# Attention into a feed-forward block on one core: the values product with its operands exchanged, a column of ones beside V, and the stages reordered

## The chip, the cores and the metric

The kernel runs on one core of one Trainium2 chip. The metric is the device time of one execution in microseconds (us), as a median of several runs. A profile of one execution tells what each engine did: TensorE (PE, with its weight loads as PEld), VectorE (DVE), ScalarE (ACT), GpSimd (POOL), and the queue of SyncE (SP), which issues transfers.

## What is computed

Eight batches, 12 heads, 448 positions, head size 64. Queries and keys are normalised, attended, the heads are joined to rows of 768, and each row goes through two products with a sine term between them.

```python
# q, k, v: (8, 12, 448, 64) f32; w_in (768, 2048), w_out (2048, 768), alpha (2048)
q_n = q / sqrt(mean(q*q, -1) + 1e-6) * g_q           # k_n likewise with g_k
scores = (q_n @ k_n^T) / 8
attn = exp(scores - max); attn /= sum(attn, -1) + 1e-9
x = (attn @ v) -> rows of 12 * 64 = 768               # 3584 rows
h = x @ w_in
out = (h + sin(alpha * h)**2 / alpha) @ w_out
```

The kernel leaves out the subtraction of the maximum before and after the change alike.

## The kernel before

**Tiling.** One batch is a stage (loop over `b`, L628). A batch's 12 heads are three groups `c` of four heads (two pairs of two). The 448 positions are cut as 64 rows x 7 (`j`), so that a tile always fills 128 partitions with two heads. A group of q and k is called `ci = 3 b + c`.

**The steps of a stage.** For each group: load q and k (`l`, L155), square them (`q`, L274, ACT for the first two groups, POOL later), sum the squares (`u`, L288, DVE), take the inverse root as Ln and Exp (`r`, L292, ACT), fold g in (`g`, L283, POOL), scale (`k`, L302, DVE for the first four groups, POOL later) and transpose to `qkT`: by PE and copies (`p`, L323) for the first groups, by DMA transposes on SP (`t`, L315) later. A token `S` is one tile of scores (L348): four 64x64 matmuls of 448 columns into a pair of PSUM banks, and one Exp on ACT into `expT`. There are 21 a stage. They hold keys on the partitions and queries along the columns.

**Values and sums.** `attend` (L385) multiplies with V (or a tile of ones, for the sums) as the weights and 448 columns of `expT` as the moving side. Its result is x already turned, head dimension on the partitions. Group 0 takes 64-column weights for the values (`v`), and for the sums (`o`) 32 columns of ones over half of the queries in batches 1 to 7 (L404). Groups 1 and 2 go together with 32-column weights: sums (`x`), even and odd columns of V (`y`, `z`; L416). The sums become reciprocals as Ln and Exp(-) on ACT (L423 to L432; group 0's halves are also moved across partitions by DVE, L429), and DVE multiplies them into `xT` (L440).

**The two products.** `first_product` (L460) multiplies the six 128-row blocks of `xT` (`kt`) by w_in, 16 blocks `m` of the 2048, 448 columns each. Its first four `m` are interleaved over the blocks in the order 0, 1, 2, 4, 3, 5. Each pair of `m` then passes `snake` (L443): Sin on ACT, square on POOL (even `m`) or ACT, and on DVE the sum into `g_sb` (L454). `second_product` (L498) of batch b - 1 runs inside stage b as fillers: it has 6 or 8 units, each of 8 fills, a fill being 8 matmuls of 64x64 weights and 384 columns in four quadrants (L548); at a unit's end DVE copies and adds (L554, L555) and SP stores. The last batch's second product runs alone at the end, on the whole array (L529).

**What sets the order.** The plans STAGE_0, STAGE_1 and STAGE_N (batches 2 to 7) are lists of tokens, written out by hand, and each engine works its instructions in that order. A number or `f` is that many fills, `f` from the second open unit. The dictionary of a plan holds tokens that are issued beside the first product, by its step (-1: within the interleaved part). A string of digits gives the pair of PSUM banks (of four) to each tile in turn. `W`, `O` and `V` are loads of w_in, w_out and V, all on POOL's queue, which casts them to bf16. An `S` with a number has that many warm-up matmuls on a blank tile before it (L352).

Of the kernel before, what the change touches and what calls it, by code (L numbers as in the profile page):

```python
# [17 lines left out]
try:  # L18
# [15 lines left out]
        "q000 u000 q010 G q011 q001 u010 g00 u011 r01 g01 D1 u001 k01 r00 k00 q11 u11 O00 q10 V00 p012 "  # L34
        "W01 q20 p00 g1 u10 r1 q21 u20 V01 g2 S4 V02 S k11 l3 k10 S1 S1 S4 W00 W02 S u21 r2 p1 L S2 S q31 "
        "S3 k21 q30 k20 D2 S S3 o3 l4 g3 S W10 W12 o1 o3 p2 u30 l5 S3 u31 S1 S W11 S4 v7 S S S q40 S S x5 "
        "y3 q41 u41 x1 g4 z4 u40 x1 r4 y4 O01 q50 z3 r3 O10 "
    ),
    "012311203203312021021302301231032103021321302",
    {-1: 'u50 O11 k30', 0: 'D4 k401', 1: 'k411', 2: 'q51', 3: 'k31 k400 u51', 5: 'k410', 7: 'g5 V12', 8: 't3 V10 V11 t4 l6 l7'},  # L40
# [3 lines left out]
        "4 r2 f f k20 1 f f 2 k21 S 1 q31 1 t2 S 1 S 2 S q30 2 S 2 S S 3 f S 3 S 1 f S 1 S 1 u31 2 l5 g3 "  # L44
        "S u30 o1 o6 1 r3 V10 2 S f q41 1 f 2 S 2 S 2 q40 S u41 1 v1 v1 S v3 V12 S k31 q50 v2 u40 S 2 S "
        "V11 g5 S z4 x7 y7 r4 z3 g4 k30 "
    ),
    "1320201203203013133213130101301231203123",
    {-1: 'u50 t3', 0: 'k41', 2: 'k40', 5: 'q51', 6: 'l6 t4', 8: 'u51 l7'},
# [3 lines left out]
        "f q40 f 1 f 2 q41 1 S 1 r2 5 f S f f S 2 S 1 u40 k20 1 k21 S 1 u41 1 S 2 S 1 q31 1 o7 1 f f 1 S "  # L53
        "t2 f 1 r4 S 2 f 1 l5 q30 S 3 S 1 u31 1 S 2 u30 g3 V10 S 2 S S k41 3 S v6 r3 k30 S k31 v1 S 2 V12 "
        "g4 2 S 2 S 2 q51 l6 S t3 z3 x7 y5 y2 z4 V11 "
    ),
    "01223131310312323203013012301021310231023",
    {-1: 'k40', 0: 't4', 2: 'q50', 3: 'u50', 4: 'u51 g5', 6: 'l7'},
)
LAST = "0123012"  # L60


def tokens_of(plan):

    return [t for word in plan.split() for t in ("F" * int(word) if word.isdigit() else [word])]
# [3 lines left out]
def kernel(  # L69
# [12 lines left out]

# [24 lines left out]
    vpool = ctx.enter_context(tc.tile_pool(name="vpool", bufs=2))  # L115
    npool = ctx.enter_context(tc.tile_pool(name="norm", bufs=2))
    tpool = ctx.enter_context(tc.tile_pool(name="qkT", bufs=8))
    epool = ctx.enter_context(tc.tile_pool(name="expT", bufs=17))
    hpool = ctx.enter_context(tc.tile_pool(name="parts", bufs=1))
    rpool = ctx.enter_context(tc.tile_pool(name="rec", bufs=2))  # L120
    xpool = ctx.enter_context(tc.tile_pool(name="xT", bufs=1))
# [6 lines left out]

# [3 lines left out]
    upcoming = deque()  # L132
# [11 lines left out]
    qk, vb, norm = {}, {}, {}  # L144

    def strip(pp, hi):

        s = 2 * hi + pp
        return slice(s * 32, s * 32 + 32)

    def half_of(c, pp, hi):

        return pp ^ (hi, 1, 0)[c]

    def load_qk(ci, k_queue=nc.sync):  # L155

# [17 lines left out]
    def load_v(b, c):  # L174


        if b not in vb:
            vb[b] = vpool.tile([P, NP, NJ, D], BF16, tag="vb", name="vb")
        heads = v[b].rearrange("(n pp) (p j) d -> n pp p (j d)", pp=2, j=NJ)
        rows = vb[b].rearrange("p n j d -> p n (j d)")  # L180
        if c == 1:
            for r in range(2):
                nc.gpsimd.dma_start(out=rows[r * 64:r * 64 + 64, 1:4], in_=heads[1:4, 1 - r].rearrange("n p x -> p n x"))
        else:
            n = slice(0, 1) if c == 0 else slice(4, NP)
            nc.gpsimd.dma_start(out=rows[:, n], in_=heads[n].rearrange("n pp p x -> (pp p) n x"))
# [15 lines left out]
    ones = const.tile([P, D], BF16)  # L202
    nc.vector.memset(ones, 1.0)
    ones_row = const.tile([1, P], F32)
    nc.vector.memset(ones_row, 1.0)
    eps = const.tile([P, 1], F32)
# [13 lines left out]
    def spread_g():  # L220

        nc.gpsimd.tensor_mul(g_rows[:, 2], g_rows[:, 0], g_rows[:, 1])
        ps = bank_pair("gps")
        nc.tensor.matmul(ps[:, 0, :D], ones_row, g_rows[:, 2], start=True, stop=True)
        nc.vector.tensor_copy(gg[:, 0], ps[:, 0, :D])
        give_back(ps)

    def spread_alpha():

        ps = bank_pair("aps")  # L230
        nc.tensor.matmul(ps[:, 0, :MT], small, ident_f32, start=True, stop=True)
        nc.vector.tensor_copy(alpha_sb[:, :, 0], ps[:, 0, :MT])
        give_back(ps)
        nc.vector.reciprocal(inv_alpha_sb, alpha_sb)

    def load_w_in(half, c):


        cols = slice(half * D_FF // 2, (half + 1) * D_FF // 2)
        rows = moe_w_in[c * 2 * P:(c + 1) * 2 * P, cols]  # L240
        nc.gpsimd.dma_start(out=w_in_sb[half][:, 2 * c:2 * c + 2],  # L241
                            in_=rows.rearrange("(p x) f -> p x f" if c else "(x p) f -> p x f", x=2))

    def load_w_out(hi, lo):
        src = moe_w_out.rearrange("(mt p) d -> p mt d", p=P)
        part = 2 * hi + lo
        mts = slice(part * MT // 4, (part + 1) * MT // 4)
        nc.gpsimd.dma_start(out=w_out_sb[:, mts], in_=src[:, mts])  # L248

    def keep_busy(n, rhs):  # L250


# [7 lines left out]
    def norm_tasks(ci):  # L260

        st = SimpleNamespace()
        early = ci <= NC
        st.ms = npool.tile([P, 2, 2 * NJ], F32, tag="ms", name="ms")
        st.inv, st.inv_ps, st.scaled = {}, [], 0
        st.sq, st.n = {}, None
# [5 lines left out]
        def square(w, heads=(0, 1)):  # L274
            if ci < 2:
                st.sq[w] = spare(2 * ci + w).rearrange("p (a d) -> p a d", d=D)
                rows = slice(heads[0] * NJ, (heads[-1] + 1) * NJ)
                nc.scalar.activation(st.sq[w][:, rows], qk[ci][:, w, rows], ACT.Square)  # L278
            else:
                st.sq[w] = npool.tile([P, 2 * NJ, D], F32, tag="sq", name="sq")  # L280
                nc.gpsimd.tensor_mul(st.sq[w], qk[ci][:, w], qk[ci][:, w])  # L281
# [10 lines left out]
        def rsqrt(ws=slice(0, 2)):  # L292
            ln = npool.tile([P, 2, 2 * NJ], F32, tag="inv", name="inv")
            inv = bank_pair("inv") if early else ln
            if early:
                st.inv_ps.append(inv)
            for w in range(2)[ws]:
                st.inv[w] = inv[:, w, :2 * NJ]
            nc.scalar.activation(ln[:, ws], st.ms[:, ws, :], ACT.Ln, scale=1.0 / D, bias=eps)
            nc.scalar.activation(inv[:, ws, :2 * NJ], ln[:, ws], ACT.Exp, scale=-0.5)  # L300

        def scale(w, heads=(0, 1)):  # L302
            eng = nc.vector if early else nc.gpsimd
# [20 lines left out]


# [22 lines left out]
    def scores(c, j, warm=0):  # L348

# [3 lines left out]
        for pp in range(2):  # L353
            for hi in range(2):
                qkt, r = qkT[2 * c + pp], slice(hi * 64, hi * 64 + 64)
                o = half_of(c % NC, pp, hi) * 64
# [6 lines left out]
    avs, recs = {}, {}  # L363
    presums = {}

    def add_tile(b):


        if b not in presums:
            presums[b] = SimpleNamespace(n=0, t=rpool.tile([P, 2, S], F32, tag="rec", name="rec"))  # L370
        s = presums[b]
        first = expT[b * NC, 0] if s.n == 0 else s.t
        s.n += 1
        nc.vector.tensor_add(s.t, first, expT[b * NC, s.n])

    def split_sum(b):

        s = presums[b]
        assert s.n == NJ - 1
        s.parts = [hpool.tile([P, 2, S], BF16, tag=f"part{i}", name="part") for i in range(2)]  # L380
        nc.vector.tensor_copy(s.parts[0], s.t)
        nc.vector.tensor_sub(s.parts[1], s.t, s.parts[0])
    STEPS = {"o": "ones 0", "v": "values 0", "x": "ones 1", "y": "low 1", "z": "high 1"}

    def attend(b, what, tiles=range(NJ)):  # L385

        kind, both = what.split()
        both = both == "1"  # L390
        if tiles[0] == 0:
            avs[what] = bank_pair("av")
        av = avs[what]
        pre = presums.get(b) if what == "ones 0" else None
        last = 1 if pre else NJ - 1
        halved = what == "ones 0" and b > 0
        for j in tiles:
            if halved:
                for hi in range(2):
                    for qh in range(2):  # L400
                        for pp in range(2):
                            r = half_of(0, pp, hi) * 64
                            r, o = slice(r, r + 64), slice((2 * pp + qh) * 32, (2 * pp + qh) * 32 + 32)
                            nc.tensor.matmul(av[o, hi, :S // 2], ones[r, :D // 2], expT[b * NC, j][r, hi, qh * S // 2:(qh + 1) * S // 2],  # L404
                                             start=(j == 0), stop=(j == NJ - 1))
                continue
            for hi in range(2):
                for c in ((1, 2) if both else (0,)):
                    for pp in range(2):
                        r = half_of(c, pp, hi) * 64  # L410
                        r = slice(r, r + 64)
                        o, k = (strip(pp, hi), c - 1) if both else (slice(pp * 64, pp * 64 + 64), hi)
                        d = slice(kind == "high", D, 2) if both and kind != "ones" else slice(D // 2 if both else D)
                        w = ones[r, d] if kind == "ones" else vb[b][r, 2 * c + hi, j, d]
                        x = pre.parts[j] if pre else expT[b * NC + c, j]
                        nc.tensor.matmul(av[o, k, :S], w, x[r, hi, :], start=(j == 0), stop=(j == last))  # L416
        if tiles[-1] < last:
            return
        if kind == "ones":
# [261 lines left out]
```

The softmax here doesn't subtract the row's maximum and nothing guards it: scores larger than these inputs give would overflow.

## Time and profile before

| | us |
|---|---|
| median of three runs | 407.25 (407.24 to 407.7) |
| span of the profiled execution, first to last instruction | 405.8 |
| PE busy in the span | 391.4 |
| ACT | 315.3 |
| POOL | 283.6 |
| DVE | 240.6 |

The profiled execution's span is counted from its first to its last instruction; the median of the runs is 1.45 us longer, and holds what lies around the span. Busy times are sums over the span. Matmuls are pipelined, so two that overlap are counted once; a start of a matmul and the start of the next tell more than its duration. The profile's page has the shares by slices of the span, groups of instructions by line, and a chain: the work that ended last, followed back from the end, each step to what released it. In the table of windows each row is a stretch of the span with the busy time of each engine. A weight load (PEld) and a matmul (PE) are separate instructions. The costliest groups are the two products (L548 148.0 us of PE, L468 147.0), the exps (L360, 143.7 us of ACT) and DVE's part of the sine term (L454, 81.1).

### The profile page before, as it was taken

What the parts mean: (1) busy time and instruction counts of PE and PEld (TensorE: products, weight loads), DVE (VectorE), ACT (ScalarE), POOL (GpSimd) and SP (SyncE); (2) the same over time, 40 slices, a digit from 0 to 9 for tenths busy, and PEclk for the clock granted to TensorE, in tenths of its full rate; (3) what the DMA queues carried; (4) which work ended last, traced back from release to release, by engine and by line L of the source; (5) the groups of instructions that cost most, each with busy time, mean ns of one, the idle gap of its engine ahead of it and who ended that gap; (6) DMA issues with size and microseconds to landing.
All of it is one profiled execution on the core that took longest, in us unless ns stands there. A gap on an engine that the chain in (4) does not pass through costs nothing.

```text
span 405.8 us, 15218 instructions
## 1 busy us (share of the span) xinstructions
PE 391.4 (96%) x6755; PEld 238.8 (59%) x6758; DVE 240.6 (59%) x364; ACT 315.3 (78%) x474; POOL 283.6 (70%) x268
## 2 busy tenths in 40 slices
PE   1999999999999999999999999999999999999996
PEld 1346467645675566755676556755667556765564
DVE  4956665756783576638584475836685485544512
ACT  5798889868896879958898678958898679877600
POOL 5998889987959789588877779597895784003300
PEclk9999999999999999999999999999999999999999
DMA  7999999855286925697076923879046901620022
GB/s 266 215 254 241 210 221 255 193 155 171 53 164 162 151 94 88 182 198 153 3 140 178 200 102 70 185 158 209 3 94 179 166 2 22 108 61 1 2 78 79
DMA packets 67846, 55.46 MB, mean 137 GB/s; under 512 B 41524, under 2 KB 63172, under 8 KB 67780
## 3 DMA queue, kind: packets, MB, share of 16 engines
q1 hardware_dynamic: 56578, 41.43, 42.2%
q0 software_dynamic: 10432, 11.81, 19.0%
q8 instruction: 53, 0.87, 0.9%
q10 hardware_dynamic: 770, 1.25, 0.9%
q14 instruction: 13, 0.11, 0.1%
HBM read 45.62 MB, written 11.01 MB: 140 GB/s over the span
## 4 chain that ended last, share of the span: by engine, by line
PE 88%; POOL 5%; DMA 3%; issue 1%; DVE 1%; ACT 1%; SPq 0%; POOLq 0%
PE hps L468 34%; PE ops L548 31%; PE av L416 9%; PE sc L357 7%; PE ops L529 5%; POOL sq L281 2%; DMA qk<-in_q_dram 2%; DMA qk<-in_k_dram 2%; PE av L404 1%; POOL qk L286 1%; POOL w_out_sb L248 1%; POOL w_in L241 1%; ACT expT L360 1%; DVE g_sb L454 0%; DVE xT L440 0%
## 5 line engine op out<-in xcount | busy, mean ns | idle before, releaser
L360 ACT ACTIVATE expT<-sc 128x896 bf16<-128x896 f32 x168 | 143.7, 917 | 7.4 <-PE sc L357 6.6
L548 PE MATMUL ops<-w_out_sb,g_sb 64*64 64x384 bf16 x3072 | 148.0, 323 | 0.0
L468 PE MATMUL hps<-xT,w_in 128*128 128x448 bf16 x768 | 147.0, 353 | 0.4 <-DVE g_sb L454 0.4
L468 PEld LDWEIGHTS <-w_in 128*128 128x128 bf16 x768 | 74.4, 98 | 72.5 <-issue 3.9
L454 DVE SCALAR_TENSOR_TENSOR g_sb<-s,inv_alpha_sb,hps 128x448 bf16<-128x448 f32 x128 | 81.1, 676 | 59.1 <-POOL s L449 58.5
L548 PEld LDWEIGHTS <-g_sb 64*64 64x64 bf16 x3072 | 91.9, 107 | 37.0 <-issue 3.8
L449 POOL TENSOR_TENSOR s<-s 128x448 f32<-128x448 f32 x64 | 59.6, 932 | 65.7 <-ACT s L446 43.9
L446 ACT ACTIVATE s<-hps,alpha_sb 128x448 f32<-128x448 f32 x128 | 73.9, 627 | 37.7 <-PE hps L468 37.2
L309 POOL TENSOR_TENSOR qkn<-qk,inv 128x448 bf16<-128x448 f32 x80 | 72.9, 938 | 24.6 <-issue 17.1
L281 POOL TENSOR_TENSOR sq<-qk 128x896 f32<-128x896 f32 x44 | 73.3, 1678 | 3.9 <-DVE ms L290 3.0
L357 PE MATMUL sc<-qkT 64*64 64x448 bf16 x672 | 60.3, 357 | 0.7 <-ACT expT L360 0.3
L286 POOL TENSOR_TENSOR qk<-qk,gg 128x896 f32<-128x896 f32 (+1 forms) x25 | 50.5, 2021 | 2.2 <-ACT g_sb L278 1.5
L554 DVE COPY osb<-ops 128x384 f32<-128x384 f32 x48 | 26.7, 556 | 38.5 <-PE ops L548 38.3
L290 DVE TENSOR_REDUCE ms<-sq 128x14 f32<-128x896 f32 x44 | 46.4, 1078 | 3.3 <-POOL sq L281 3.2
L440 DVE TENSOR_TENSOR xT<-av,rec 128x896 bf16<-128x896 f32 (+1 forms) x26 | 25.7, 1016 | 26.8 <-ACT rec L432 21.4
L451 ACT ACTIVATE s<-s 128x448 f32<-128x448 f32 x64 | 36.9, 577 | 2.9 <-DVE g_sb L454 0.7
L416 PE MATMUL av<-expT,vb 64*32 64x448 bf16 (+1 forms) x1120 | 38.1, 350 | 0.0
L357 PEld LDWEIGHTS <-qkT 64*64 64x64 bf16 x672 | 21.7, 107 | 13.8 <-issue 6.7
L555 DVE TENSOR_TENSOR osb<-osb,ops 128x384 f32<-128x384 f32 x48 | 26.6, 554 | 1.7
L416 PEld LDWEIGHTS <-vb 64*32 64x32 bf16 (+1 forms) x1120 | 20.8, 96 | 11.0 <-issue 2.2
L429 DVE TENSOR_REDUCE rec<-rec 32x448 f32<-32x448 f32 x28 | 17.1, 610 | 9.7 <-ACT rec L425 9.4
L529 PE MATMUL ops<-w_out_sb,g_sb 128*128 128x384 bf16 (+1 forms) x144 | 21.0, 309 | 0.0
(51 smaller groups left out, 185.8 us busy)
## 6 DMA issues: line engine op xcount, KB each, us to landing
qk<-in_q_dram SPq DMA_DIRECT2D x23, 448.0 KB, 5.2
qk<-in_k_dram SPq DMA_DIRECT2D x23, 448.0 KB, 5.7
out_dram<-osb SPq DMA_DIRECT2D x45, 192.0 KB, 2.9
w_out_sb<-in_moe_w_out_dram POOLq DMA_DIRECT2D x4, 768.0 KB, 12.8
w_in<-in_moe_w_in_dram POOLq DMA_DIRECT2D x6, 512.0 KB, 12.2
vb<-in_v_dram POOLq DMA_DIRECT2D x16, 168.0 KB, 7.2
vb<-in_v_dram POOLq DMA_DIRECT2D x8, 224.0 KB, 5.3
out_dram<-osb SPq DMA_DIRECT2D x13, 96.0 KB, 4.3
```

What stands on the lines that cost most here:

```text
L281: nc.gpsimd.tensor_mul(st.sq[w], qk[ci][:, w], qk[ci][:, w])
L286: nc.gpsimd.tensor_mul(x, x, gg.to_broadcast([P, len(heads) * NJ, D]))
L290: nc.vector.reduce_sum(st.ms[:, w, rows], st.sq[w][:, rows], axis=AX.X)
L309: eng.tensor_mul(n[:, :, hi, :], x[:, hi], inv[:, hi].unsqueeze(2).to_broadcast([P, NJ, D]))
L357: nc.tensor.matmul(sc[o:o + 64, hi, :S], qkt[r, 1, j * REST:(j + 1) * REST], qkt[r, 0, :], start=True, stop=True)
L360: nc.scalar.activation(expT[c, j], sc[:, :, :S], ACT.Exp, scale=SCALE)
L416: nc.tensor.matmul(av[o, k, :S], w, x[r, hi, :], start=(j == 0), stop=(j == last))
L446: nc.scalar.activation(s1, hps, ACT.Sin, scale=alpha_sb[:, m, :])
L449: nc.gpsimd.tensor_mul(s2, s1, s1)
L454: nc.vector.scalar_tensor_tensor(g_sb[:, m, (b % 2) * S:(b % 2 + 1) * S], s2, inv_alpha_sb[:, m, :], hps, op0=ALU.mult, op1=ALU.add)
L468: nc.tensor.matmul(ps[:, m % 2, :S], w_in_sb[m * 2 // MT][:, kt, m % (MT // 2) * P:(m % (MT // 2) + 1) * P], x[:, kt, :], start=(kt == ORD ...
L548: nc.tensor.matmul(st["ps"][os, r, :HALF], g_sb[rs, m, c0 + o * 64:c0 + o * 64 + 64], w_out_sb[rs, m, half * HALF:(half + 1) * HALF], star ...
```

## The change

The values product exchanges its operands. A 64x64 block of `expT` (keys by queries) is now the weights, and V with a column of ones beside it, 65 columns, is the moving side. The result has queries on the partitions: 64 columns of x and their sum as column 65. One `v` token is one tile `j`: 28 matmuls. All of `attend` with its sums is gone, and with it ACT's Ln and Exp on them. DVE takes the reciprocal of the sums and multiplies. x must then be turned: by a DMA transpose on SP (`T`, batch 1 for groups 0 and 1, batches 2 to 7 for all) or by 7 PE transposes and a copy (`P`, batch 0, and group 2 of batch 1). V is loaded in fp32 on SP's queue and cast into place by DVE (`C`) or POOL (`c`).

The first product is opened early: `H` takes a pair of banks and does the blocks 0 to 3 of two `m`; blocks 4 and 5, those of group 2, come when the stage's plan is through. w_in's row order is plain again. w_out is loaded in four parts by column half and row half, all of them now after w_in, and the second product of batch 0 does all first halves before the second ones, storing each apart. A square can go to the other engine (`Q`), an inverse root can stay out of PSUM so that POOL scales (`R`). All plans are written anew; the warm-up matmuls are fewer.

```diff
 STAGE_0 = (
     (
...
+        "q010 q000 V00 G u000 u010 g00 q011 q001 g01 u011 u001 r01 V02 R00 q10 k00 q11 k01 g1 u10 u11 Q20 "
+        "p012 p00 r1 c00 Q21 S S k10 S k11 u20 S2 W00 D1 g2 u21 S p1 r2 S S1 v v S v W02 l3 V01 W01 k20 D2 v "
+        "v S k21 c01 v v S W11 S1 W10 p2 S P00 l4 C02 S S q40 S v u40 v v S2 v q41 u41 v v S1 q30 q31 v V11 "
+        "S1 u30 S1 u31 v v v v S v W12 l5 D4 S g3 P10 V10 v v r3 H P21 H k31 O00 k30 L p3 q50 u50 O01 O10 C10 "
+        "C11 O11 Q51 "
     ),
...
 STAGE_N = (
     (
...
+        "2 S f f q41 f q40 f 1 r2 u41 k20 2 k21 f S 2 V10 1 S l5 1 t2 S 3 S 2 S 1 v 1 S 1 v S v 2 S v S v v v "
+        "f 2 u40 S 1 f T0 2 C10 q30 S 1 r4 1 V12 1 S 1 S 2 g3 g4 S k41 1 q31 v 1 v S 1 v v k40 S v v S 1 v T1 "
+        "1 S 1 S V11 2 v S 1 v v u30 f v v f v v f T2 f f 1 q50 u31 f f 2 r3 H k31 k30 C12 H t3 g5 u50 "
     ),
...
     def load_v(b, c):
...
+        vs[b, c] = vpool.tile([P, 2, NJ, D], F32, tag="vs", name="vs")
+        heads = v[b].rearrange("(n pp) (p j) d -> n pp p (j d)", pp=2, j=NJ)[2 * c:2 * c + 2]
+        nc.sync.dma_start(out=vs[b, c].rearrange("p n j d -> p n (j d)"), in_=heads.rearrange("n pp p x -> (pp p) n x"))
+
+    def cast_v(b, c, eng):
+        src = vs.pop((b, c)).rearrange("p n j d -> p (n j) d")
+        eng.tensor_copy(v_ones[b % 2][:, 2 * c:2 * c + 2, :, :D].rearrange("p n j d -> p (n j) d"), src)
...
-    def load_w_out(hi, lo):
+    def load_w_out(half, part):
         src = moe_w_out.rearrange("(mt p) d -> p mt d", p=P)
...
+        cols = slice(half * HALF, (half + 1) * HALF)
+        mts = slice(part * MT // 2, (part + 1) * MT // 2)
+        nc.gpsimd.dma_start(out=w_out_sb[:, mts, cols], in_=src[:, mts, cols])
...
+    def values(b, c, j):
+        if j == 0:
+            avs[b, c] = bank_pair("av")
+        av = avs[b, c]
+        e = expT.pop((b * NC + c, j))
+        for i in range(NJ):
+            for o in range(2):
+                hi, jq = divmod(2 * i + o, NJ)
+                for pp in range(2):
+                    r = slice(pp * 64, pp * 64 + 64)
+                    nc.tensor.matmul(av[o * 64:o * 64 + 64, pp, i * W:(i + 1) * W], e[r, hi, jq * REST:(jq + 1) * REST],
+                                     v_ones[b % 2][r, 2 * c + hi, j], start=(j == 0 and i == 0), stop=(j == NJ - 1 and i == NJ - 1))
+        if j < NJ - 1:
             return
...
+        sums = av[:, :, :NJ * W].rearrange("p pp (i w) -> p pp i w", w=W)
+        rec = npool.tile([P, 2, NJ, 1], F32, tag="rec", name="rec")
+        nc.vector.reciprocal(rec, sums[:, :, :, D:])
+        xn[b, c] = npool.tile([P, NJ, 2, D], BF16, tag="xn", name="xn")
+        nc.vector.tensor_mul(xn[b, c].rearrange("p i pp d -> p pp i d"), sums[:, :, :, :D], rec.to_broadcast([P, 2, NJ, D]))
+        give_back(avs.pop((b, c)))
+
+    def turn(b, c):
+        x = xT[b, c] = xpool.tile([P, 2, S], BF16, tag="xT", name="xT")
+        nc.sync.dma_start_transpose(out=x.rearrange("p k s -> p (k s)").rearrange("p (i t) -> p i t", t=P),
+                                    in_=xn.pop((b, c)).rearrange("p i pp d -> p (i pp d)"))
+
+    def pe_turn(b, c, act):
+        tp = bank_pair("xt", BF16)
+        src = xn.pop((b, c))
+        for i in range(NJ):
+            nc.tensor.transpose(tp[:, 0, i * P:(i + 1) * P], src[:, i].rearrange("p pp d -> p (pp d)"), ident)
...
+    def open_product(b):
+        i = len(opened)
+        opened[i] = bank_pair("hps")
+        for m in (2 * i, 2 * i + 1):
+            multiply(b, i, m, range(KT - 2))
+
     def first_product(b, beside):
...
+        for task in beside.get(-1, ()):
+            task()
+        EARLY = len(opened)
+        for m in range(2 * EARLY):
+            multiply(b, m // 2, m, range(KT - 2, KT))
...
             units = [[(i, half)] for i in order for half in range(2)]
+            if b == 0:
+                units = units[::2] + units[1::2]
```

## The prediction

> **What bounds the kernel now.** I read the table of time windows first, because the page's shares (PE 96%, ACT 78%) are means over unlike stages. Columns: window, length, busy time of PE, weight loads (PEld), DVE, ACT, POOL, granted clock, DMA share, GB/s.
>
> ```profile
> 0.00:35.85 35.85, 25.62 (x421) 12.96 (x425) 22.43 (x40) 27.96 (x42) 30.84 (x36) 1.00 1.00 247
> ...
> 100.20:381.70 281.50, 281.50 (x5283) 174.80 (x5272) 170.84 (x255) 232.08 (x345) 195.54 (x177) 1.00 0.55 113
> 381.70:405.80 24.10, 20.61 (x143) 13.25 (x141) 5.96 (x9) 1.54 (x3) 0.93 (x1) 0.99 0.25 66
> ```
>
> From 100.2 to 381.7 us, the six stages of batches 2 to 7, PE is never idle: 281.50 of 281.50, at full clock. ACT has 232 of it, DVE 171, POOL 196. So there only PE time counts, until another chain becomes late. Before 35.85 PE is not the bound: DMA is at 1.00 and PE idles or runs warm-up matmuls. The chain of waits then prices one stage (start, length, what):
>
> ```profile
> 99.96 2.40 PE ops L548 x56
> ...
> 109.86 0.80 PE av L404 x56
> ...
> 119.64 1.14 PE av L416 x24
> ...
> 124.51 4.10 PE av L416 x168
> 128.61 18.27 PE hps L468 x96
> 146.88 2.40 PE ops L548 x56
> ```
>
> The period is 146.88 - 99.96 = 46.92 us. First product: 18.27. Second product: 56 fills of 8 matmuls, 0.65 us per 16 elsewhere in this view, so 0.325 a fill, 18.2. Scores: 21 tiles at 0.19, 4.0. The rest is what the change replaces: sums of pair group 0 (L404) 0.80, its values 28 at 1.14/24 = 1.33, sums and values of groups 1 and 2 4.10: **6.2 us**.
>
> **Part by part.**
>
> *Values product (PE).* Per stage 21 tiles x 28 = 588 matmuls, each with its own weight load, 64x64, 65 moving columns, four quadrants side by side. No row has this form, so bounds. Below: the second product streams 384 columns in four quadrants in 0.65 us/4 = 162.5 ns, 0.423 ns a column; 65 columns take 27.5 ns for four, 6.9 ns each, 588 x 6.9 = 4.0 us. Above: the nearest row with short streams and a weight load each is L404, 0.80 us/56 = 14.3 ns, though its 224 columns alone need 11.8 of those; 588 x 14.3 = 8.4 us. What decides is whether weight loads hide and whether instructions come fast enough. On loads, the transposes of stage 0 are the nearest row, with short streams behind 128-column weights:
>
> ```profile
> 17.52 0.89 PE L334 MATMUL tp<-ident,qkn 64*128 64x64 bf16 x28
> ```
>
> 28 in 0.89 us, the last lasting 0.24, in two row halves side by side: about 0.65/13 = 50 ns a step, near 128 columns x 0.423 = 54 and below 128 + 64 columns (81). So a load runs during the matmul before it; 64 columns need 27 ns, no more than the stream. Do four quadrants load at once? At the first second-product matmuls after L404:
>
> ```profile
> L548 PE MATMUL ops<-w_out_sb,g_sb x16: 322/323/348, 110.6 to 111.1; 64*64 64x384 bf16 x16
> ```
>
> The maximum, 348, is that of the first four, which stand behind exposed loads: 26 ns over 322, one load and not two; in the single starts all four quadrants begin their second matmul 186 ns after their first. So loads do run side by side. On supply: in L404's block the first starts are 2 to 5 ns apart, but once the queue's reserve is used the weight loads follow at 8 to 9 ns. I take 7.9 ns, between 7.5 (the stream with a little loss) and 8.5 (supply): 588 x 7.9 = 4.65 us. **Gain 6.2 - 4.65 = 1.55 us a stage**, ends +2.2 (slower) and -2.2.
>
> A rule speaks against this. The Trainium skill, "TensorE: Matmul & The Clock Gate", section "Wait — 56ns, not 53.3ns?", says that matmul starts never come closer than about 25 ns however few the columns. The starts 2 to 5 ns apart in L404's block contradict it across quadrants; it may hold within one, where 27 ns hide it. Were it true of all, 588 x 25 = 14.7 us, 8.5 us a stage lost, about +60 us in all. The skill's "PSUM — Partial Sum Buffer", section "Specifications (TRN2)", names 8-byte cachelines; blocks of 65 fp32 start off such a line every second time, and no run here shows what that costs.
>
> *Normalising.* Gone: Ln and Exp on ACT, 0.93 + 0.95 + 0.54 + 2 x 0.58 = 3.6 us a stage, and DVE's four moves, 4 x 0.61. New on DVE: three reciprocals (L234, 128x16: 0.25), three multiplies at the old price (L440: 1.09, as now), three casts of V (between 0.62, the bf16 copy L341, and 1.09). DVE goes from 29.2 to about 30 us, ACT from 38.8 to 35, both under 45: hidden by PE. Without that cover the casts would cost up to 3.3 us.
>
> *V loads* move from POOL's queue to SP's, in fp32: POOL loses 4 issues x 0.67 a stage; SP gains 3 x 0.5 us and three transposes at 1.25 us issue each, beside some 19 us of issuing in a stage (201 to 232 us): free while no load sits before a late transpose. A V load waits on SP for a buffer that a cast frees; behind it wait stores and T. In the plans each cast is well ahead, so nothing.
>
> *Turning x back.* In batches 2 to 7 it is a DMA transpose as large as one of today's (64x1792 against 128x896 elements). The critical one is T2. After the last `v` come 8 fills (2.6 us) and two H (16 x 190 ns = 3.05): **5.65 us of cover**. Chain: last matmul 0.25, reciprocal 0.25, multiply 1.09, issue 0.1, transpose. Before it on SP stand only a V load and T1, both issued; no store is left between.
>
> ```profile
> qkT<-qkn SPq DMA_TRANSPOSE x42, 4.8
> ```
>
> Single ones took 3.1 to 10 us, those in quiet stretches (156, 203, 251, 344 us) 4.5 to 4.8. With 4.5 the chain is 6.2: **PE waits 0.5 us a stage** (ends: none with 3.1; 6 us with 10). Batch 1 uses P21: 7 transposes of 128 columns, 0.4 us; its chain (1.6, 0.4, a copy of 0.9) lies under H.
>
> *Reordered first product.* Same 96 matmuls: none.
>
> *Stage 0.* ACT runs from 13.9 us to the last exp at 33.8 nearly without a gap; the first product starts at 35.6. Gone from it: 1.9 us of Ln/Exp among the exps, and the 1.8 us tail of sums behind the last one. Two squares (0.94 each) come over from POOL, beside the 2.2 us that ACT now waits before the first exp. So the first product could start up to 3.4 us earlier. Against it: w_in's later parts are issued behind casts and squares on POOL (now issued at 27.7 to 29.9, landing 11 to 14.5 us later, with the DMA full); one part 2 to 3 us late would cost as much. All of w_out moves behind w_in, where one part went first: 6 us of a full DMA are freed. I take -1.5, ends -3.4 and +2.
>
> **The sum**, on the profiled execution's span of 405.8 us. Stage 0: -1.5. Stage 1: -1.55 + 0.4 = -1.15. Batches 2 to 7: 6 x (-1.55 + 0.5) = -6.3. Tail: none; the last 144 matmuls are the same. Together -8.95: 396.85. The runs' median, 407.25, lies 1.45 above the span; I keep that: **398.3 us**.
>
> **Rivals.**
> 1. *Short matmuls are not that cheap* (supply or loads): slower. The profile's hint is L404 at 14.3 ns; against it, 11.8 of that is stream. At 14.3: -1.5 + (2.2 + 0.4) + 6 x (2.2 + 0.5) = +17.3, 424.5. It decides from where the sum is zero: -1.5 + 0.4 + 3.0 + 7x = 0, x = -0.27, 5.95 us, 10.1 ns a matmul.
> 2. *T2 is late*: PE waits for x at each stage's end. For: transposes behind loads took 6 to 10 us. Against: only one V load is near. With 7: chain 8.7, wait 3.0: -2.65 + 6 x 1.45 = +6.05, 413.3. It decides from a wait of 2.0 us, a transpose of 6.0.
> 3. *The freed PE time is not used*: stage 0 stays with its loads, and later stages wait for exps or banks. ACT's exps follow at 0.84 us, 21 x 0.84 = 17.6, plus 1.6 for the norms and 2.6 of sines and table load, 21.8 of the about 27 us before the first product: room, but the last exp stands only 1 us before its `v`. It gives 403 to 407.
> 4. *More is won*: 7 ns a matmul, no wait, stage 0 at -3.4: -3.4 - 1.7 - 6 x 2.1 = -17.7, 389.5.
>
> **Chances.** Forecast (392 to 403) 0.60; rival 1 0.12; rival 2 0.09; rival 3 0.12; rival 4 0.07. The range 390 to 412 takes in the forecast, rival 3 and half of rival 4, and reaches to the milder forms of 1 and 2: about 0.8. A measurement tells 0.2% (0.8 us) from no change. Faster: forecast, rival 4 and most of 3, 0.75; same 0.05; slower 0.20.
>
> **What would show it.** The period of a middle stage: 45.9 (45.4 without waits for x); 49 or more is rival 1, with PE still full; 48 with an idle PE before `hps`, ended by the transpose of x, is rival 2. Row by row: `av` 588 a stage in 4.0 to 5.0 us; SP's transposes to xT landing in 4 to 5; ACT near 35 a stage; first `hps` in stage 0 before 35. I am wrong if `av` takes over 10 ns each, if an engine other than PE ends most waits, or if the first product of batch 0 starts later than now.

## The result, and the profile after

| us | before | after |
|---|---|---|
| median of four runs each | 407.48 (407.24 to 407.89) | 500.19 (499.14 to 503.89) |
| span of the profiled execution | 405.8 | 497.4 |
| PE busy | 391.4 | 412.2 |
| matmuls on PE, each with a weight load | 6755 | 9513 |
| packets on the instruction queue | 53 (0.87 MB) | 74 (1.21 MB) |

The ratio is 1.2286, with a 95% interval of 1.224 to 1.2331. The forecast was 398.3, its range 390 to 412: wrong in sign and far outside.

The same windows as before, by the stages of the changed kernel (up to the first product of batch 0; batches 2 to 7; the tail), with the same columns:

```profile
0.00:48.10 48.10, 27.11 (x782) 16.99 (x783) 23.93 (x40) 28.02 (x41) 33.14 (x40) 0.87 1.02 253
125.70:472.80 347.10, 294.54 (x7298) 199.77 (x7297) 176.84 (x262) 213.88 (x314) 185.93 (x157) 0.96 0.50 113
472.80:497.40 24.60, 21.04 (x146) 13.53 (x143) 6.39 (x10) 1.74 (x3) 0.93 (x1) 0.97 0.26 65
```

In the middle window PE was full before; now it is idle for 52.6 us of 347.1, at a clock of 0.96. No other engine has become full: ACT has 214 of 347, DVE 177. The tail is what it was. So the loss is in stages 0 to 7, and PE loses it without another engine being the bound. The waits of the page (engine, line, what ended the idle time, us in total, times, longest) say what PE waited for:

```profile
DVE rec L363 <- PE av L357: 89.1, 24, 7.2
...
PEld L357 <- issue: 55.6, 36, 3.8
PE av L357 <- issue: 51.1, 32, 3.7
...
PE ops L493 <- issue: 13.8, 6, 4.4
```

DVE waits for PE. PE's own idle time ends by "issue": no semaphore, no transfer of the kernel's data, no bank. The places of the stops tell that its next instruction was not there. The chain, in the middle of a stage (start, length, what), shows where:

```profile
205.58 0.22 PE av L357 x28
...
206.32 0.06 PE av L357 x7
206.37 2.21 issue
208.58 0.58 PE av L357 x49
...
211.03 0.10 PE av L357 x7
211.13 0.91 issue
212.04 0.49 PE av L357 x21
...
213.17 0.37 PE sc L338 x4
```

A tile of 28 short matmuls takes 0.22 us, 7.9 ns each, exactly the price predicted. Then, in the middle of a tile, PE stops for 2.21 us, and a little later for 0.91. Counting PE's weight loads and matmuls one by one in the trace, the stops of this stage come behind instruction 7361, 7617, 7873, 8129 and 8641: always 256 or a multiple apart. Of the gaps over 0.5 us between two matmul starts after the first 20 us, 39 stand at that place in a row of 256. They hold 78.5 us, 2.0 on average and 4.74 at most. Before there was none at such a place: its three gaps of that length end by exps on ACT and a sum on DVE.

256 instructions are 128 pairs of weight load and matmul. They fit one packet of the instruction queue: 1.21 MB by 74 is 16 KB, 64 bytes for each of 256. Below, such a packet's instructions are called a piece, and the place between two pieces a boundary.

```profile
q8 instruction: 74, 1.21, 1.0%
```

The single packets show the loop. PE comes through a boundary at 208.58; the next packet starts at 209.74, 1.16 us later, and takes 1.04; at 210.89 PE issues its last matmul of the piece, and it resumes at 212.04, 1.26 us after the packet's end. At the other stops the packet started 0.4 to 4.4 us after the boundary and took up to 2.4, and the end of the packet was mostly some 1.4 us ahead of the resumption. The queue is idle most of the time (74 packets of about 1 us in 497): what limits is a chain of delays for each piece, not bytes.

The clock adds to it. At 213.17 four matmuls of the scores take 0.37 where they took 0.19:

```profile
PE   1668997699966999779968799859987699978997
...
PEclk9985898899989899989998999999998999979999
```

Granted clock at half speed: 54.5 us in 11 stretches, against 2.7 us before. The last one lies at the end of the run, like the 2.7 us before; the other ten are 3.4 us long or multiples of it. PE was busy in 45.5 us of them, so they cost at most half of that, 22.7 us. The Trainium skill, "TensorE: Matmul & The Clock Gate", section "What's actually happening", states that the array falls to half rate after an idle window of about 3.4 us. The lengths of the stretches here agree with that figure, but the idle need not last that long: the half clock from 209.39 to 216.22 came after a stop of 2.21 us, with PE busy for 1.20 of the 3.41 us ahead of it.

**Where the 91.5 us of span are.** Measured from the last matmul of one first product to that of the next: batch 0 ends at 69.8 for 54.1 (+15.6), batches 1 to 7 take 402.9 for 327.0 (+75.9), the tail 24.7 for 24.7.

### The profile page after: what moved, and what is told of

The parts are those of the page before. It is cut to its first block, busy times and chain, and to the rows that moved or that the text cites. A ratio compares the mean times of both kernels' runs of the same rounds, so it can differ in the third digit from the quotient of the medians.

```text
span 497.4 us, 20773 instructions
## 1 busy us (share of the span) xinstructions
PE 412.2 (83%) x9513; PEld 272.4 (55%) x9513; DVE 253.0 (51%) x379; ACT 297.8 (60%) x441; POOL 264.1 (53%) x238
## 3 DMA queue, kind: packets, MB, share of 16 engines
q8 instruction: 74, 1.21, 1.0%
## 4 chain that ended last, share of the span: by engine, by line
PE 70%; issue 16%; ACT 5%; POOL 4%; DVE 3%; DMA 2%; POOLq 0%; DVEq 0%; ACTq 0%
PE ops L493 24%; PE hps L409 22%; PE av L357 10%; PE sc L338 8%; PE ops L476 4%; POOL s L392 2%; POOL qkn L293 2%; DVE g_sb L397 2%; ACT expT L341 1%; DMA qk<-in_q_dram 1%; ACT s L389 1%; PE sc L333 1%; ACT L578 1%; DMA qk<-in_k_dram 1%; ACT s L394 1%
## 5 line engine op out<-in xcount | busy, mean ns | idle before, releaser
L493 PE MATMUL ops<-w_out_sb,g_sb 64*64 64x384 bf16 x3072 | 171.8, 342 | 14.2 <-issue 13.8
L493 PEld LDWEIGHTS <-g_sb 64*64 64x64 bf16 x3072 | 103.4, 113 | 41.2 <-issue 16.9
L357 PE MATMUL av<-v_ones,expT 64*64 64x65 bf16 x4704 | 68.2, 200 | 51.1 <-issue 51.1
L357 PEld LDWEIGHTS <-expT 64*64 64x64 bf16 x4704 | 64.3, 113 | 62.9 <-issue 55.6
L264 POOL TENSOR_TENSOR sq<-qk 128x896 f32<-128x896 f32 x38 | 63.5, 1679 | 39.1 <-DVE ms L273 33.5
L338 PE MATMUL sc<-qkT 64*64 64x448 bf16 x672 | 70.5, 387 | 6.9 <-issue 4.7
L363 DVE RECIPROCAL rec<-av 128x14 f32<-128x14 f32 x24 | 5.9, 246 | 89.1 <-PE av L357 89.1
L394 ACT ACTIVATE s<-s 128x448 f32<-128x448 f32 x64 | 36.9, 577 | 4.7 <-DVE g_sb L397 0.9
L338 PEld LDWEIGHTS <-qkT 64*64 64x64 bf16 x672 | 25.7, 114 | 23.3 <-issue 17.7
L283 ACT ACTIVATE inv<-ms,eps 128x28 f32<-128x28 f32 (+1 forms) x25 | 7.8, 313 | 35.5 <-DVE ms L273 35.5
L365 DVE TENSOR_TENSOR xn<-av,rec 128x896 bf16<-128x896 f32 x24 | 26.2, 1092 | 0.8
```

Of the source, the lines that this page charges most:

```text
L264: nc.gpsimd.tensor_mul(st.sq[w][:, rows], x, x)
L338: nc.tensor.matmul(sc[o:o + 64, hi, :S], qkt[r, 1, j * REST:(j + 1) * REST], qkt[r, 0, :], start=True, stop=True)
L357: nc.tensor.matmul(av[o * 64:o * 64 + 64, pp, i * W:(i + 1) * W], e[r, hi, jq * REST:(jq + 1) * REST], v_ones[b % 2][r, 2 * c + hi, j], st ...
L493: nc.tensor.matmul(st["ps"][os, r, :HALF], g_sb[rs, m, c0 + o * 64:c0 + o * 64 + 64], w_out_sb[rs, m, half * HALF:(half + 1) * HALF], star ...
```

## The experiments

Two theories. **Supply**: PE's instructions come one piece of 256 at a time, and a piece takes 3.5 to 4.5 us to arrive; a stretch that uses a piece faster stands still. **Array**: a 64x64 weight load with 65 columns in four quadrants costs some 20 ns by itself (588 in one stage, batch 3, took 12.68 us from each start to the next, with the stops between them: 21.6 ns each), and "issue" is only how the profile shows it. A1 to A5 start from the kernel after, B1 to B4 from the kernel before, M1 and M2 are streams alone.

The table gathers what the arguments use. Pairs are those of one stage outside its first product; the period is the median of batches 2 to 7; stops are gaps over 0.5 us at a boundary (after the first 20 us), with their number and their sum.

| kernel | pairs (pieces) | period us | stops, us | time us |
|---|---|---|---|---|
| before | 784 (6.1) | 46.9 | 0 | 407.48 |
| after | 1120 (8.75) | 58.0 | 39, 78.5 | 500.19 |
| A1 fewer | 760 (5.9) | 46.2 | 9, 11.6 | 412.89 |
| A2 whole | 784 (6.1) | 56.2 | 19, 37.8 | 484.78 |
| A3 spread | 1120 (8.75) | 57.4 | 41, 68.5 | 498.85 |
| A4 spread, some whole | 1036 (8.1) | 56.5 | 39, 66.6 | 492.49 |
| A5 spread, all whole | 784 (6.1) | 52.9 | 12, 22.0 | 466.88 |
| B1 split | 1232 (9.6) | 55.2 | 42, 52.8 | 465.59 |
| B2 whole | 448 (3.5) | 50.8 | 0 | 432.7 |
| B3 quarter | 896 (7.0) | 47.0 | 3, 4.7 | 412.74 |
| B4 half | 1008 (7.9) | 48.3 | 11, 12.6 | 422.32 |

The kernel before stood at 408.77 beside A1, A2, B1 and B2, 408.31 beside A3, A4, M1 and M2, and 408.26 beside A5, B3 and B4. Only B3 and B4 have intervals; the others are one execution each, and no difference below some 5 us among them is used.

### B1: more instructions for the kernel before, the same work

```diff
-                        nc.tensor.matmul(st["ps"][os, r, :HALF], g_sb[...], w_out_sb[rs, m, half * HALF:(half + 1) * HALF], ...)
+                        for p in range(2):
+                            w = half * HALF + p * HALF // 2
+                            nc.tensor.matmul(st["ps"][os, r, p * HALF // 2:(p + 1) * HALF // 2], g_sb[...], w_out_sb[rs, m, w:w + HALF // 2], ...)
```

> The kernel before, with each second-product matmul of 384 columns cut into two of 192, each with its own weight load; same result, same order, 448 more matmuls a stage (1328 instead of 880). Theory supply: 1232 of them lie in the 28.65 us outside the first product, 9.6 pieces of 128 at about 4 us, 38 us; stages of 55 to 58 us instead of 46.9, time 465 to 490, with idle of PE put down to issue at every 256th instruction. Theory array: two streams of 82.5 ns for one of 162.5, 0.3 us a stage, time 409 to 412. Theory order: as array.

465.59 us, a loss of 56.8, with no short matmul of 65 columns anywhere: the lower end of supply's range, far from array's. The same signs come up (waits of this kernel):

```profile
PEld L550 <- issue: 35.1, 49, 1.8
PE ops L550 <- issue: 23.8, 31, 1.5
```

42 stops, again all at one place in a row of 256. The clock stays at 0.995, so this loss is supply alone. The period of 55.2 less 18.3 for the first product is 36.9, over 9.6 pieces: 3.8 us each.

### B2: the kernel before with fewer instructions

```diff
-                for r in range(2):
-                    for o in range(2):
...
+                nc.tensor.matmul(st["ps"][:, 0, :HALF], g_sb[:, m, c0:c0 + P], w_out_sb[:, m, half * HALF:(half + 1) * HALF], ...)
...
-                    nc.vector.tensor_add(osb[:, 0], osb[:, 0], st["ps"][:, 1, :HALF])
```

> The kernel before with the same whole-array second product (544 matmuls a stage instead of 880). Prices the drains alone. Theory supply: before is not held by supply (PE never idle), so only the drains count: 3 to 5 us a stage, time 430 to 445. If before were held by supply already, it would be under 407.

432.7, and no stops. It prices what A2, A4 and A5 pay for the same edit: matmuls on the whole array between scores in quadrants cost 3.9 us a stage (50.8 for 46.9), as the chain shows: scores 0.31 where they were 0.19, and four whole-array matmuls (two fills) 0.76 where four alone stream 0.65.

```profile
108.75 0.31 PE sc L357 x4
109.06 0.76 PE ops L545 x4
```

### A1: the kernel after with most values matmuls left out

```diff
-        for i in range(NJ):
+        for i in range(NJ) if j in (0, NJ - 1) else (0,):
```

> The changed kernel, but of each tile's 28 matmuls of the values product only 4 are made, except in a group's first and last tile (left out: most of the sum over keys). Matmuls a stage: 3 x (28 + 28 + 5 x 4) = 228 for values instead of 588, in all 856, as many as the kernel before had (880). Theory supply (TensorE's instructions arrive in pieces of 256, 128 weight loads and 128 matmuls; the piece after the next is asked for when one is begun and takes 3.4 to 5.5 us, so short matmuls run the reserve dry): no idle of PE put down to issue within the values product, clock back at full, time 375 to 400. Theory array (the short matmuls and their writes are slow themselves, at 7.9 ns or a bit more each): the removed 360 a stage give back 2.8 us a stage, 23 in all, time 470 to 480. Theory order (the new plans wait for other engines): the waits stay, time above 450.

412.89: 13 us above supply's range, with nine stops left, and far from array's 470 to 480. Array could explain a gain of 360 x 21.6 ns = 7.8 us a stage; the period fell by 11.8, because the stops inside other lines' work go too. It also shows what stays lost when supply doesn't limit. Stage 0 begins its first product at 34.50, 1.1 us earlier than before, but ends it at 56.8 for 54.1: a stop at the second boundary (29.4 to 31.6) set the clock to half from 33.2 to 40.1. Later stages now wait here and there for other engines (PE's scores for exps, 5.4 us in all, and for the transposes of q and k, 4.0). Even with most of the values product gone, the reordered kernel isn't ahead of the one before.

### A2: the kernel after with whole fills

The edit of B2 on the kernel after: 336 pairs fewer in a stage.

> The changed kernel, with the second product's four 64x64 matmuls of a step made as one of 128x128 on the whole array (162 ns either way by the rows of before) and no add of two halves on DVE; same result. Matmuls a stage 112 instead of 448 there, 880 in all, with the whole values product kept. Theory supply: the stalls shrink to few, though each change between 64x64 and 128x128 work drains the array (0.1 us, some 40 a stage): 49 to 52 us a stage, time 420 to 445. Theory array or order: the values product stays as slow, plus the drains: 500 to 530.

484.78: a miss. The stops are half (37.8 us for 78.5), but not gone, although a stage now needs no more pieces than before. I put that down to order: 588 pairs of the values stand close together, with fewer pairs between. A3 was made to test that.

### M1 and M2: the pairs by themselves

M1 issues runs of pairs in four quadrants, with nothing else in the kernel; M2 has 192 loads of q and k beside them.

```diff
+    for o, w, m in quads(256, 65):
+        nc.tensor.matmul(o, w, m, start=True, stop=True)
...
+    for o, w, m in quads(128, 384):
+        nc.tensor.matmul(o, w, m, start=True, stop=True)
```

> None of the work: matmul streams alone, with no transfers beside them (the output is left out but for one tile). Streams of 64x64 quadrants, each with its own weight load, behind 48 long matmuls each: 1024 with 65 columns, 1024 with 192, 512 with 384, 96 with 65; then 512 whole-array ones of 128 columns. Theory supply: a piece of 128 pairs takes at least 3.2 to 3.6 us however short they are, beyond the first one or two. So 1024 of 65 columns take 20 to 27 us (array 7.7), 1024 of 192 about the same (array 21), 512 of 384 their array time, 21, without idle, the 96 short ones under 1.5 us, the 512 of 128 columns 28. Theory array: 65 columns 20 us or more too, but as even starts 20 ns apart and no gaps, and 96 short ones 1.9 us.

> The same streams with 192 loads of 224 KB running beside them on SP's queue (again the output is left out but for one tile). Theory supply: pieces come by transfer too, so each takes longer beside loads, 4 to 6 us: 1024 of 65 columns take 28 to 45 us, and 512 of 384 columns (a piece lasts 5.2 us on the array) begin to show gaps. Theory array: as without the loads.

The timeline of M1 on PE (start, length, form, count, and the idle time before with what ended it):

```profile
14.59 1.64 PE L67 MATMUL a<-x 64*64 64x65 bf16 x175
18.58 1.24 PE L67 MATMUL a<-x 64*64 64x65 bf16 x128 [2.35 <-issue]
22.04 1.98 PE L67 MATMUL a<-x 64*64 64x65 bf16 x128 [2.21 <-issue]
25.49 1.98 PE L67 MATMUL a<-x 64*64 64x65 bf16 x128 [1.48 <-issue]
...
91.55 20.99 PE L73 MATMUL a<-x 64*64 64x384 bf16 x512
...
122.94 0.98 PE L76 MATMUL a<-x 64*64 64x65 bf16 x96
```

This settles it. 175 pairs run at 8.3 ns (1.64 less the last one's own 0.19), then PE gets exactly 128 at a time, every 3.64 us on average (18.58 to 40.40, six pieces): 28 ns a pair. The 1024 took 27.1 us, just over the 20 to 27 that supply foretold. From 20.55 on PE has half its clock, which is why 128 pairs then last 1.98 us and not 1.24; the next piece still comes 3.45 to 4.0 us after the last, as at full clock (18.58 to 22.04), so the clock isn't what limits. 96 short pairs, fewer than a piece, run straight through. Pairs of 384 columns, 41 ns each, use a piece in 5.25 us and never stop. With loads beside (M2):

```profile
18.93 1.98 PE L71 MATMUL a<-x 64*64 64x65 bf16 x128 [3.74 <-issue]
24.02 1.98 PE L71 MATMUL a<-x 64*64 64x65 bf16 x128 [3.12 <-issue]
...
103.49 20.99 PE L77 MATMUL a<-x 64*64 64x384 bf16 x512
```

4.46 us a piece (18.93 to 45.68), 35 ns a pair; the 1024 took 33.5 us, within the forecast. I had expected stops at 384 columns here; there were none.

The single packets of M1 make the loop plain: PE passes a boundary at 18.58, the next packet starts 1.05 us later and takes 0.96, and PE resumes 1.44 us after it: 3.45 us, in which nothing else is fetched.

### A3: is it the order? Values spread out

STAGE_N was rewritten: each tile of the values stands alone between fills and scores.

```diff
-        "2 S f f q41 f q40 f 1 r2 u41 k20 2 k21 f S 2 V10 1 S l5 1 t2 S 3 S 2 S 1 v 1 S 1 v S v 2 S v S v v v "
...
+    "F F f f q41 f q40 F S r2 u41 F S k20 F F k21 F F F S F F S V10 F l5 S v F F S v F S v t2 F F S v F S v ... ",
...
-        slot = int(upcoming.popleft())
+        slot = free_at[0]
```

> The changed kernel with the plan of batches 2 to 7 written anew: same work and matmul count, but the 21 values tiles stand one by one between fills and scores from the fifth score tile to the end, and banks are taken in the order in which they come free; batches 0 and 1 keep their plans. Theory supply: the mean need outside the first product is 1120 matmuls, 8.75 pieces, in 27 us of array time, 3.1 us each, a little over what is supplied (3.4 to 5), while about 1.5 pieces lie ready from the first product: stages of 46 to 52 us instead of 57 to 58, time 435 to 465. If peaks did not matter, or the short matmuls were slow themselves: no change, 490 to 510.

498.85, where I expected 435 to 465: order isn't it. The stops move into the fills and stay, 41 of them, 68.5 us. The period of 57.4 less 18.3 is 39.1 over 8.75 pieces, 4.5 us each: the mean need of the stage outside its first product is what counts.

### A4 and A5: spread, with fewer instructions

A4 takes 14 of the 56 fills of a stage whole, those beside the first product; A5 all of them.

```diff
+                if mode["whole"]:
+                    nc.tensor.matmul(st["ps"][:, 0, :HALF], g_sb[:, m, c0:c0 + P], w_out_sb[...], ...)
+                else:
                     for r in range(2):
...
```

> As the spread plan, and 14 of the 56 fills of a stage, the 6 just behind the first product and the 8 just ahead of the next, made on the whole array (2 matmuls instead of 8), where they bring no more mode changes; 1036 matmuls outside the first product instead of 1120. Theory supply: 1 to 3 us a stage less than the spread plan alone, stages of 45.5 to 49, time 425 to 450. Theory array or order: no different from the spread plan.

> The spread plan with all fills of batches 2 to 7 on the whole array (112 matmuls a stage instead of 448), so 784 outside the first product, as many as before, evenly spread; batches 0 and 1 keep their plans and their second product comes out whole too. Theory supply: 6.1 pieces in about 31 us (27 of array time and 4 of mode changes): 5 us each, above the 4.5 that a piece took beside this kernel's transfers: stalls nearly gone, stages 49 to 52 us (57 to 58 now, 56 with whole fills but the old plan), time 445 to 465. Theory array or order: the stages stay at 56 or more.

A4, 492.49, missed: 8.1 pieces are still too many, at 4.7 us each. A5 came to 466.88, just above its range. It needs no more pieces than the kernel before, and from batch 2 on it has five stops at a boundary, 5.1 us together; its period of 52.9 is B2's 50.8 and 2.1 us, in which first products also wait for xT. So at the lower need the order does matter (A2's 56.2 against 52.9), and at the higher one it doesn't (58.0 against 57.4).

### B3 and B4: where does the limit begin?

The kernel before, with B1's cut in every fourth, and in every second, step of a fill.

```diff
+                        parts = 2 if m % 4 == 1 else 1
```

> The kernel before with every fourth step of the second product cut in two (112 more matmuls a stage, 896 instead of 784 outside the first product). Theory supply: 7.0 pieces of 128 in 28.7 us of array time, 4.1 us each, still above the 3.8 that a piece took in the kernel with all steps cut: no more than 0.5 us a stage, time 408 to 412. Theory array: 0.1 us a stage, 408.

> The kernel before with every second step cut (224 more a stage, 1008 outside the first product). Theory supply: 7.9 pieces at 3.8 us are 30 us against 28.8 of array time, and some unevenness: 1.2 to 3 us a stage, time 416 to 430, with stalls at every 256th instruction. Theory array: 0.2 us a stage, 409.

B3: 412.74, ratio 1.0114 (1.0084 to 1.0145), just above its range; B4: 422.32, ratio 1.0336 (1.0292 to 1.0381), within it. At 7.0 pieces in a stage, 28.7 us outside the first product, hardly anything shows in batches 2 to 7 (47.0 for 46.9). At 7.9 the period grows, by 1.4 us. Batch 1 begins to lose earlier. B3 has 816 pairs there (6.4 pieces, where before had 720 in 27.3 us) and takes 50.5 us for 45.5, with two stops at a boundary of 4.1 us in all and one stretch of half clock; B4 takes 53.5. The DMA's share is 0.85 there in B3, 0.66 in batch 2. So the limit is no fixed number of pieces in a stage. The kernel before, at 6.1 pieces in 28.6 us, 4.7 each, stood just on the safe side.

## Why the prediction was wrong

**The step that failed** is the one on supply: "in L404's block the first starts are 2 to 5 ns apart, but once the queue's reserve is used the weight loads follow at 8 to 9 ns. I take 7.9 ns". The 8 to 9 ns are right as a rate within a piece (8.3 in M1, 7.9 in the kernel). They were taken for the rate that can be kept up. L404's block has 56 pairs, less than half a piece, so it could not show the other limit: 128 pairs in 3.6 to 4.5 us, 28 to 35 ns a pair, on average over everything outside the first product. The term "588 x 7.9 = 4.65 us" should not have been priced by itself: 336 pairs more a stage are 2.6 pieces, and with the need already at 4.7 us a piece, each costs about its full price; 2.6 x 4.5 = 11.8 us by M2's or A3's rate. The period grew by 11.1.

**Rival 1** named supply, with a chance of 0.12, but priced it from the same block, at 14.3 ns (424.5 us), and said "with PE still full". PE isn't full: it idles by "issue". Two lines of before bear on it and weren't used: the instruction queue's 53 packets beside 13,513 PE instructions, one packet for some 256; and so one packet for every 4.7 us of a stage outside its first product. How fast they can follow each other, before doesn't show; its closest two start 3.38 us apart. As an upper bound that is 26 ns a pair, far above 14.3.

```profile
q8 instruction: 53, 0.87, 0.9%
```

**The rule weighed against the change.** The 25 ns floor between matmul starts of the Trainium skill's "TensorE: Matmul & The Clock Gate", section "Wait — 56ns, not 53.3ns?", is contradicted for four quadrants by M1's 8.3 ns. The estimate worked out from it, 60 us lost, came nearer than mine for another reason: the average that supply allows, 28 to 35 ns, happens to lie near that figure. That was luck. Another page states the mechanism: "Runtime: NRT & Kernel Launch", section "Instruction fetch mechanics", has instructions refilled in blocks of 16 KiB, which hold 256 of them, and calls the cost of crossing a block mostly hidden. The block agrees with the positions counted here. The cost does not: 78.5 us of stops in this kernel.

**What was right.** A reciprocal took 0.246 us (0.25), a multiply 1.092 (1.09). A cast of V on DVE took 1.156 on average, above the bound of 1.09 (its median was 0.95), and was hidden. ACT fell from 315.3 to 297.8. PE had no wait that V's loads ended. **x turned back** in time:

```profile
L409 PE MATMUL hps<-xT,w_in x768: 349/353/582, 48.1 to 472.6; 128*128 128x448 bf16 x192
L370 SPq DMA_TRANSPOSE xT<-xn x20: 1222/1244/1887, 94.6 to 453.6; - x20
...
DMA to landing us min/median/max: 2.9/3.0/5.1
```

The transposes landed in 3.0 us, not 4.5, and no first product waits for xT (0.2 us of idle time before all 768): the 0.5 us a stage of the sum fell away here, and rival 2 with it. It says little of a PE that doesn't stop: in A5, where PE is quicker, first products wait for xT 2.9 us in all, some 0.5 a stage. The first product itself was unchanged.

**Stage 0** was forecast 1.5 us earlier and came 12.5 later (48.1 for 35.6). A1, with the same plan and few values matmuls, starts at 34.50, within 0.4 us of the forecast, although two stops of 0.90 and 2.04 us are left in it; so the new order of the stage doesn't account for the 12.5. Five stops undid it, of 3.67, 0.46, 3.68, 1.59 and 0.71 us, 10.1 in all, with half the clock for 17.1 us of the stage, its first product included:

```profile
25.21 0.38 PE L357 MATMUL av<-v_ones,expT 64*64 64x65 bf16 x11 [3.67 <-issue]
...
37.33 0.58 PE L357 MATMUL av<-v_ones,expT 64*64 64x65 bf16 x49 [3.68 <-issue]
...
48.06 3.17 PE L409 MATMUL hps<-xT,w_in 128*128 128x448 bf16 x8
```

**What is open.** A piece takes 3.8 us in B1 and B4 but 4.5 in the kernel after and in A3. Half clock accounts for part of it at most (45.5 us of busy time at half rate, up to 2.8 us of a stage's 39.7). What varies at the stops is the time from the boundary to the packet's start: 1.1 us on average in M1, 2.0 in M2, 1.8 in B1, 1.9 in the kernel after, while the packet itself takes 1.0 to 1.1 on average and PE resumes mostly 1.4 after it. Loads beside made a piece slower in M2; whether the transposes of x or V's larger loads are what delays the packets in the kernel after was not tried. Nor does any run here show why a packet starts a microsecond or more after a boundary.

## What to carry to other kernels

Count PE's instructions as well as its columns: for every stretch between long streams, divide the pairs of weight load and matmul by 128, and compare with the time at some 3.6 to 4.5 us a piece (this chip, these kernels); B3's batch 1 lost time at a need of 4.3. A rate read from a block of less than 128 pairs is a burst, not what can be kept up. When PE is idle by "issue" and the stops lie 256 instructions apart, fewer and longer matmuls help, and another order helps only if the mean need is met.

## What the runs showed of the hardware that was not expected

- Pieces of 256 PE instructions arrive one at a time: 3.64 us a piece alone, 4.46 beside loads; the queue's 1.0% share hides it.
- A stop can cost twice: PE at half clock for 51.2 us in the kernel after, 3.4 in B1, whose stops are shorter (1.3 us on average for 2.0), the stretch at the end of each run left out. A stop of 2.2 us was enough to bring it on.
- Changing between the whole array and quadrants costs some 0.1 us each time: 3.9 us a stage in B2.
